# Seven products for four in the y w_in stage, weight scales by block, another order: a single-core chain of linear attention, a gated product and SoLU with layer norm

## The chip, the cores and the metric

The kernel runs on one core of a Trainium2 chip. The core has TensorE (matmuls, from SBUF into the eight banks of PSUM), VectorE, ScalarE, GpSimd and a queue for DMAs on SyncE; they run side by side and wait for each other by semaphores. The profile calls them PE (its weight loads PEld), DVE, ACT, POOL and SP. The metric is the device time of one execution in microseconds (us).

## The reference, cut to what matters

Decaying linear attention over 2 x 8 heads gives x, 1536 tokens by 512; then two dense stages follow:

```python
a = x @ w_a                      # 512 -> 1536
b = x @ w_b
y = (a * b) @ w_out              # 1536 -> 512
h = y @ w_in                     # 512 -> 1024
e = np.exp(h - h.max(-1, keepdims=True))
solu = h * e / (e.sum(-1, keepdims=True) + 1e-9)
ln = (solu - mean) / np.sqrt(var + 1e-6) * g_ln
out = ln @ moe2_w_out            # 1024 -> 512
```

Inputs and output are float32.

## The kernel before, in words

Every dense operand is scaled by a power of two and split in a high and a low half of 16 bits; a product is three matmuls, high by high, high by low and low by high (`mm3`, L139). The tokens are 12 chunks of 128, in three blocks t of 512 (four token blocks j each).

The parts of the work are generators, named by a letter, that issue a few instructions and yield. `ORDER`, a string of 1228 words, resumes them one by one; since all five queues are issued by hand, this string is the order of every engine. The letters: G a load, A scores, K and Q decays, C the products of a chunk, O and T its state, X the scale of a pair of chunks, Y their split; D decodes a block of weights (two ScalarE passes, a VectorE pass `fab`, then its largest magnitudes `st_ab`), P makes a scale out of these, S splits the block (ScalarE the high half, VectorE the low half `wab`). A scale is a spread of the largest values by matmuls (`pm`) and three short VectorE instructions (`pow2`).

The products x w_a and x w_b run for two feature blocks of each pair as plain products (L: banks `pa`, `pb`, 24 groups of 12 matmuls of 512 columns in all; one L is halved to 256 columns), and for the other four pairs by Strassen's scheme with seven products (R: banks `rA`, `rB`, `rC`, on sums of halves of x, `tt` and `xt`, and of the weights, H and E, `ws`). One scale for w_a and one for w_b serve a pair of feature blocks, so a plain block waits until both blocks of its pair are decoded.

M is (a b) w_out (bank `py`, 432 matmuls of 512 columns). U makes the scale of y for a block t, V splits it: `halve` reads the bank on ScalarE and again on VectorE. N (`L3`) makes h for a token block in two banks `ph`, 4 x 3 matmuls each, 288 of 512 columns for the 12 token blocks, and goes on with softmax and norm: VectorE finds the largest value in both banks (L601), ScalarE takes the exponential, VectorE multiplies by h out of the banks (L616), takes moments (L619, L621), GpSimd works out the inverse root (L625 to L630), VectorE applies it (L633). Z splits the result and turns it (by DMA, for the last two blocks by TensorE), W multiplies by the last weights (bank `po`) and stores.

PSUM has eight banks, taken in turn by all of these (`bank`). A tile that is still read keeps its bank, and the matmul that gets the bank next waits for it.

Of the kernel before, what the change touches and what calls it, by code (L numbers as in the profile page):

```python
# [756 lines left out]
```

## Time and profile before

| | us |
|---|---|
| median of 3 runs (least to most) | 462.25 (461.88 to 462.25) |
| the profiled execution | 462.19 |
| its span, first to last instruction | 460.4 |
| TensorE busy | 443.3 |
| VectorE, ScalarE, GpSimd busy | 316.7, 221.5, 179.7 |

The profiled execution agrees with the median to 0.06 us; 1.8 us of it lie outside the span. Engine times in the page are merged busy times; a matmul's duration there is longer than the step to the next one, because matmuls overlap, so the price of a matmul is read from the chain of waits (time of a run of them by their number).

### The profile page before, as it was taken

Reading aid. Unit: us, or ns where it says so; the run is one execution under the profiler, and the core shown is the slowest. Engines: PE = TensorE matmul, PEld = TensorE weight load, DVE = VectorE, ACT = ScalarE, POOL = GpSimd, SP = SyncE. Lnnn points to the kernel's source line nnn. Section 1 sums busy time; section 2 is a strip of 40 time slices with the busy share of each in tenths; the row PEclk is TensorE's granted clock in tenths of the full one; section 3 lists DMA queues with packets and bytes.
Section 4 is the critical chain, followed back from the end, with each engine's and each line's share of the span. In section 5 each row is a group of like instructions: output and inputs, shape, how many; then the busy total and the mean of one; then the engine's idle time right before and its main releaser. Section 6 shows DMA issues by size and latency. Waiting matters only on the chain.

```text
span 460.4 us, 7751 instructions
## 1 busy us (share of the span) xinstructions
PE 443.3 (96%) x3102; PEld 274.5 (60%) x3102; DVE 316.7 (69%) x572; ACT 221.5 (48%) x361; POOL 179.7 (39%) x221
## 2 busy tenths in 40 slices
PE   5777999999999999999999999999999999999996
PEld 5666645568887865888874444444444445544442
DVE  5898898799766337887798668287926799533710
ACT  1546564458536545897796354033503244322421
POOL 5756368547825505337325100003430142803230
PEclk9998999999999999999999999999999999999999
DMA  8974535650000013313606430001320020523051
GB/s 312 374 312 192 230 116 216 219 229 2 0 3 0 1 49 135 113 72 107 244 16 236 167 145 1 0 2 40 43 57 0 24 46 24 151 56 91 1 159 46
DMA packets 30371, 48.73 MB, mean 106 GB/s; under 512 B 22272, under 2 KB 22528, under 8 KB 27008
## 3 DMA queue, kind: packets, MB, share of 16 engines
...
## 4 chain that ended last, share of the span: by engine, by line
PE 90%; DVE 6%; ACT 2%; issue 1%; DMA 1%; POOL 1%; SPq 0%; ACTq 0%; DVEq 0%
PE py L139 20%; PE po L139 14%; PE ph L139 14%; PE rA L139 13%; PE rB L139 7%; PE pa L139 6%; PE pb L139 6%; PE rC L139 3%; PE px L235 2%; PE pss L214 2%; PE px L229 1%; DVE fab L337 1%; DVE sc L219 1%; DMA qk<-in_qk_dram 1%; ACT xh L284 1%
## 5 line engine op out<-in xcount | busy, mean ns | idle before, releaser
L139 PE MATMUL py<-g,wo 128*128 128x512 f16 x432 | 94.3, 379 | 0.0
L139 PEld LDWEIGHTS <-wab 128*128 128x128 f16 x744 | 71.9, 98 | 35.5 <-issue 1.1
L139 PEld LDWEIGHTS <-wo 128*128 128x128 f16 x432 | 42.2, 98 | 50.3
L139 PE MATMUL ph<-wi,yh 128*128 128x512 f16 x288 | 63.9, 379 | 0.0
L139 PE MATMUL po<-wo,zT 128*128 128x512 f16 (+1 forms) x312 | 62.9, 363 | 0.0
L139 PEld LDWEIGHTS <-ws 128*128 128x128 f16 x576 | 55.9, 98 | 7.8 <-DVE ws L437 0.7
L625 POOL TENSOR_SCALAR st<-st 128x1 f32<-128x1 f32 x12 | 3.4, 285 | 125.9 <-DVE st L621 125.8
L139 PEld LDWEIGHTS <-zT 128*128 128x128 f16 x312 | 30.5, 98 | 31.7
L139 PEld LDWEIGHTS <-yh 128*128 128x128 f16 x288 | 28.1, 98 | 33.2
L541 POOL TENSOR_TENSOR g<-c,g 128x512 f16<-128x512 f32 x24 | 31.2, 1314 | 35.2 <-ACT g L539 35.1
L608 ACT ACTIVATE e<-ph,st,ch 128x512 f32<-128x512 f32 x24 | 18.4, 773 | 43.7 <-DVE st L603 31.8
L139 PE MATMUL rA<-xt,ws 128*128 128x256 f16 x288 | 35.4, 273 | 0.0
L139 PE MATMUL pa<-xh,wab 128*128 128x512 f16 (+1 forms) x156 | 33.3, 363 | 0.0
L139 PE MATMUL pb<-xh,wab 128*128 128x512 f16 (+1 forms) x156 | 33.3, 363 | 0.0
L497 ACT ACTIVATE p<-rA 128x512 f32<-128x512 f32 x36 | 21.3, 598 | 19.9 <-PE rA L139 19.7
L335 ACT ACTIVATE raw<-raw 128x1024 f32<-128x1024 f32 x26 | 29.8, 1146 | 0.0
L648 POOL TENSOR_TENSOR zr<-e,zr 128x512 f16<-128x512 f32 x20 | 23.3, 1189 | 14.5 <-ACT zr L644 10.2
L601 DVE TENSOR_REDUCE st<-ph 128x1 f32<-128x512 f32 x24 | 16.0, 682 | 17.5 <-PE ph L139 17.5
L110 DVE TENSOR_REDUCE ym<-py 128x1 f32<-128x512 f32 x12 | 8.3, 689 | 26.1 <-PE py L139 26.1
L689 ACT ACTIVATE ob<-po,glm 128x512 f32<-128x512 f32 (+1 forms) x13 | 8.5, 655 | 30.7 <-PE po L139 23.0
L530 POOL TENSOR_TENSOR c<-p,p 128x512 f32<-128x512 f32 x12 | 16.9, 1409 | 14.4 <-ACT p L497 14.4
L382 ACT ACTIVATE yh<-py,sy 128x512 f16<-128x512 f32 x12 | 7.3, 688 | 31.3 <-DVE sy L130 31.3
(129 smaller groups left out, 765.0 us busy)
## 6 DMA issues: line engine op xcount, KB each, us to landing
...
zT<-zr SPq DMA_TRANSPOSE x20, 2.8
...
```

The source lines that it names most:

```text
L110: nc.vector.tensor_reduce(out=dst, in_=src, axis=AX.X, op=ALU.max, apply_absolute_value=True)
L139: nc.tensor.matmul(o, w[a], x[b], start=start and i == 0, stop=stop and i == 2, skip_group_check=True)
L214: nc.tensor.matmul(pss[e][:, a * P:(a + 1) * P], t[r, 1, a], t[r, 0, a], start=True, stop=True, skip_group_check=True)
L235: nc.tensor.matmul(o[r, a * P:(a + 1) * P], v[:, 2 * a + e], sc[n][e][:, a], start=(c == 0 and a == 0), stop=True, skip_group_check=True)
L335: nc.scalar.activation(hi.bitcast(F32), hi.bitcast(F32), AF.Prelu, scale=2.0 ** -112, alpha=2.0 ** 32)
L497: nc.scalar.activation(r, o, AF.Copy, scale=2.0 ** -28)
L530: nc.gpsimd.tensor_sub(c1[:, 1], p167, p5)
L541: nc.gpsimd.tensor_sub(g[:, 1], c[:, :, 0], g[:, 0])
L601: nc.vector.tensor_reduce(out=st[:, z:z + 1], in_=ph[z], axis=AX.X, op=ALU.max)
L608: nc.scalar.activation(e[z], ph[z], AF.Exp, bias=st[:, 2:3], scale=c, accum_out=st[:, 3 + z:4 + z])
L648: nc.gpsimd.tensor_sub(lo, e[z], hi)
L689: nc.scalar.activation(ob, po, AF.Copy, scale=scl["glm"][:, KB:])
```

## The change

- `L3(t, i)` now makes h for two token blocks, 2i and 2i+1, together: y by halves of its 512 features and pairs of token blocks, w_in by halves, seven products of 6 matmuls in three banks `hA`, `hB`, `hC`, in place of 2 x 24 matmuls. There are 6 of these. Three partial results per pair are copied out by ScalarE (`kept`), two are joined by VectorE (`h`), one by GpSimd (`h22`). The even block's h is then a tile in SBUF; of the odd block's one half is in SBUF, the other stays in the bank `hA`.
- `norm(t, j)` is the rest of the former `L3`. For the even block it works on 1024 columns at once.
- y is written out by ScalarE in float32 (`yf`), split by ScalarE and GpSimd (`yh`), added up by GpSimd (B, `sums_y`) and the sums split by ScalarE and VectorE (F, `yt`). The sums of w_in are made and split once (I and k, `si`, `wsi`).
- The plain pairs 0 and 1 of w_a and w_b get a scale for each feature block (p, `scale_f`), with tables twice as long, and the two blocks of w_out for them are split by halves.
- 22 matmuls on a constant are issued first on TensorE (`warm`).
- Some scales are made with a top of 12 in place of 14. `ORDER` has 1330 words and is another string throughout.

```diff
-ORDER = ("G,qk,1 G,qk,0 G,qk,6 G,kv,1 G,kv,0 G,qk,3 G,kv,3 G,qk,4 G,ab,2 G,ab,1 G,qk,2 G,kv,2 G,qk,5 A,1 A,0 A,1 A,1 Q,6 A,6 A,0 K,1 C,1 A,0 K,1 A,6 C,0 C,1 K,0 "
+ORDER = ("G,qk,0 G,kv,0 G,qk,1 G,ab,0 G,kv,1 G,qk,2 G,kv,2 G,qk,3 G,kv,3 G,ab,1 G,qk,4 G,kv,4 G,qk,5 G,kv,5 A,0 K,0 K,0 A,0 T,0 A,0 C,0 T,0 O,2 A,1 C,0 D,ab,0 "
...
+WARM = 22
...
+    pw = bank("warm")
+    for _ in range(WARM):
+        nc.tensor.matmul(pw[:, :P], identb, identb, start=True, stop=True, skip_group_check=True)
...
-        amax(stab[:, f // 2, :, f % 2] if nm == "ab" else wst[nm][:, f], x)
-        yield
+        amax(stab[:, f // 2, f % 2] if nm == "ab" else wst[nm][:, f], x)
+        yield
+    def scale_f(f):
+        return pow2(stab[:, f // 2, f % 2], 2, sab[:, :, f], TOP)
...
-            amax(r2, stab[:, f])
-            yield
-            yield from pow2(r2, 2, sab[:, :, f], TOP)
+            amax(r2, stab[:, f].rearrange("p e z -> p z e"))
+            yield
+            yield from pow2(r2, 2, sab[:, :, 2 * f], TOP)
...
-        yield from pow2(r, 1, s)
+        yield from pow2(r, 1, s, TOP if nm == "i" else 14)
...
+            k = 2 * len(PLAINW)
+            both = sab[:, 0, k:].rearrange("p (f e) z -> p f e z", e=2)
+            nc.vector.tensor_copy(both[:, :, 1], both[:, :, 0])
...
+        if nm == "i" or nm == "o" and f not in PLAINW:
+            s = scl["ro"][:, 2 * f:2 * f + 1] if nm == "o" else scl[nm][:, 0]
...
-        ss = sab[:, 0, f // 2] if nm == "ab" else scl["glm"][:, 2 * f:2 * f + 2]
+        ss = sab[:, 0, f if f // 2 in PLAINW else f - f % 2] if nm == "ab" else (scl["ro"] if nm == "o" else scl["glm"])[:, 2 * f:2 * f + 2]
...
-        ys[t] = [t_k("yh", (P, 2, 2, W), F16) for _ in range(2)]
-        yield from pow2(r, 1, s)
+        yield from pow2(r, 1, s, TOP)
...
     def split_y(t, d):
-        return halve(pys.pop((t, d)), sy[t][:, 0], ys[t][d // 2][:, d % 2])
+        if t not in yf:
+            yf[t] = [t_k("yf", (P, 2, W)) for _ in range(2)]
+        f = yf[t][d // 2][:, d % 2]
+        nc.scalar.activation(f, pys.pop((t, d)), AF.Copy, scale=sy[t][:, 0])
+        yield
+        if t not in ys:
+            ys[t] = [t_k("yh", (P, 2, 2, W), F16) for _ in range(2)]
+        c = slice(0, W if d // 2 else W // 2)
+        y = ys[t][d // 2][:, d % 2]
+        nc.scalar.copy(y[:, 0, c], f[:, c])
+        yield
+        nc.gpsimd.tensor_sub(y[:, 1, c], f[:, c], y[:, 0, c])
+        yield
+    yfs, yt = {}, {}
+    def halves(x):
+        return [x[..., k * (W // 2):(k + 1) * (W // 2)] for k in range(2)]
+    def sums_y(t):
+        (y11, y21), (y12, y22) = (halves(yf[t][h]) for h in range(2))
+        yfs[t] = [t_k("yu", (P, 2, W))]
+        u = halves(yfs[t][0])
+        nc.gpsimd.tensor_add(u[0], y21, y22)
+        yield
+        nc.gpsimd.tensor_sub(u[1], u[0], y11)
+        yield
+        yfs[t].append(t_k("yv", (P, 2, W)))
+        v = halves(yfs[t][1])
+        nc.gpsimd.tensor_sub(v[0], y11, y21)
+        yield
+        nc.gpsimd.tensor_sub(v[1], u[1], y12)
+        yield
+    def split_ys(t, k):
+        src = yfs[t][k]
+        if t not in yt:
+            yt[t] = {}
+        y = yt[t][k] = t_k("yt", (P, 2, 2, W), F16)
+        nc.scalar.copy(y[:, :, 0], src)
+        yield
+        nc.vector.tensor_sub(y[:, :, 1], src, y[:, :, 0])
+        yield
+    ifs = [None] * 4
+    def sums_i(k):
+        ifs[k] = t_k("si", (P, 2, W))
+        for r in range(2):
+            def w(h, z):
+                return fw["i", 2 * h + r][:, z]
+            if k == 0:
+                nc.gpsimd.tensor_sub(ifs[0][:, r], w(0, 0), w(0, 1))
+            elif k == 1:
+                nc.gpsimd.tensor_add(ifs[1][:, r], w(1, 1), ifs[0][:, r])
+            elif k == 2:
+                nc.gpsimd.tensor_sub(ifs[2][:, r], w(1, 1), w(0, 1))
+            else:
+                nc.gpsimd.tensor_sub(ifs[3][:, r], w(1, 0), ifs[1][:, r])
+            yield
+    def split_si(k):
+        src = ifs[k]
+        w = wt["si", k] = t_k("wsi", (P, 2, 2, W), F16)
+        s = scl["i"][:, 0]
+        nc.scalar.activation(w[:, :, 0], src, AF.Copy, scale=s)
+        yield
+        nc.vector.scalar_tensor_tensor(out=w[:, :, 1], in0=src, scalar=s, in1=w[:, :, 0], op0=ALU.mult, op1=ALU.subtract)
+        yield
...
-    def L3(t, j):
+    hs, sts = {}, {}
+    def L3(t, i):
         y = ys[t]
...
+        def product(o, y, c, w, start, stop):
+            for r in range(2):
+                wh, wl = w(r)
+                mm3(o, (y[:, r, 0, c], y[:, r, 1, c]), (wh, wl), start and r == 0, stop and r == 1)
...
+        A, Bk = bank("hA"), bank("hB")
+        product(A, y[0], at[0], wi(0, 0), True, False)
+        yield
+        product(Bk, yt[t][0], ss[0], si(0), True, False)
+        yield
+        p1 = kept("p1", A)
+        yield
+        product(A, yt[t][0], ss[1], si(1), False, False)
+        yield
+        p5 = kept("p5", Bk)
+        yield
+        product(Bk, yt[t][1], ss[1], wi(1, 1), False, True)
+        yield
+        p16 = kept("p16", A)
+        yield
+        product(A, yt[t][1], ss[0], si(2), False, False)
+        yield
+        h = t_k("h", (P, 2, W))
+        nc.vector.tensor_sub(h[:, 1], p16, Bk)
+        yield
+        C = bank("hC")
+        product(C, y[1], at[0], wi(1, 0), True, True)
+        yield
+        p167 = kept("p167", A)
+        yield
+        product(A, y[1], at[1], si(3), False, True)
+        yield
+        nc.vector.tensor_add(h[:, 0], p1, C)
+        hs[t, 2 * i] = h
+        yield
+        r = t_row("h22", (P, W))
+        nc.gpsimd.tensor_sub(r, p167, p5)
+        hs[t, 2 * i + 1] = (A, r)
+        yield
+    def norm(t, j):
         ch = scl["ch", t, j]
         c, cn = ch[:, 0:1], ch[:, 1:2]
-        js = slice(place(t, j) * P, (place(t, j) + 1) * P)
-        ph = [bank(f"ph{z}") for z in range(2)]
         st = sm.tile([P, 16], F32, name="st")
-        for z in range(2):
-            for kk in range(KD):
-                w = wt["i", kk * 2 + z]
-                mm3(ph[z], (y[kk // 2][:, kk % 2, 0, js], y[kk // 2][:, kk % 2, 1, js]), (w[:, 0], w[:, 1]), kk == 0, kk == KD - 1)
-            yield
-        for z in range(2):
-            nc.vector.tensor_reduce(out=st[:, z:z + 1], in_=ph[z], axis=AX.X, op=ALU.max)
-            if z == 1:
-                nc.vector.tensor_scalar(st[:, 2:3], st[:, 0:1], st[:, 1:2], cn, op0=ALU.max, op1=ALU.mult)
+        h = hs[t, j]
+        whole = j % 2 == 0
+        zs_ = [slice(0, 2)] if whole else [0, 1]
+        src = [h] if whole else h
...
+        for z, x in zip(zs_, src):
+            k = 0 if whole else z
+            nc.scalar.activation(e2[:, z], x, AF.Exp, bias=st[:, 2:3], scale=c, accum_out=st[:, 3 + k:4 + k])
+        yield
+        if whole:
+            nc.vector.tensor_scalar(st[:, 5:6], st[:, 3:4], 1e-9, None, op0=ALU.add)
+        else:
+            nc.vector.scalar_tensor_tensor(out=st[:, 5:6], in0=st[:, 3:4], scalar=1e-9, in1=st[:, 4:5], op0=ALU.add, op1=ALU.add)
...
+        for z, x in zip(zs_, src):
+            nc.vector.scalar_tensor_tensor(out=e2[:, z], in0=e2[:, z], scalar=st[:, 7:8], in1=x, op0=ALU.mult, op1=ALU.mult)
...
+        for z in [slice(0, 2)] if whole else range(2):
+            nc.vector.tensor_scalar(e2[:, z], e2[:, z], st[:, 8:9], r, op0=ALU.subtract, op1=ALU.mult)
+            if whole or z == 1:
...
-             "D": decode, "P": scale_w, "S": split_w, "J": sums_x, "H": sums_w, "E": split_s, "R": R1, "L": L1, "M": L2, "U": scale_y, "V": split_y, "N": L3, "Z": Z, "W": L4}
+             "D": decode, "P": scale_w, "p": scale_f, "S": split_w, "J": sums_x, "H": sums_w, "E": split_s, "R": R1, "L": L1, "M": L2, "U": scale_y, "V": split_y, "B": sums_y, "F": split_ys, "I": sums_i, "k": split_si, "N": L3, "n": norm, "Z": Z, "W": L4}
```

How the change stands on the engines, at three places. VectorE in the head of the kernel, in front of the first low half of a plain weight block, before (`xh` and `tt`: splits and sums of x; `sab`: weight scales):

```order
L337 SCALAR_TENSOR_TENSOR fab<-raw,fab 128x1024
L110 TENSOR_REDUCE st_ab<-fab 128x2
L110 TENSOR_REDUCE r_480<-st_ab 128x2
L288 SCALAR_TENSOR_TENSOR xh<-px,sx_400,xh 128x2x128 x2
L127 TENSOR_REDUCE pm<-pm 128x2
L129 TENSOR_SCALAR pm<-pm 128x2
L130 TENSOR_SCALAR sab<-pm 128x2
L260 TENSOR_TENSOR state<-old,pst 128x256
L110 TENSOR_REDUCE xst<-px 128x1
L406 SCALAR_TENSOR_TENSOR wab<-fab,sab,wab 128x512 x2
```

and with the change:

```order
L313 SCALAR_TENSOR_TENSOR tt<-px,sx_363,tt 128x256
L297 SCALAR_TENSOR_TENSOR xh<-px,sx_271,xh 128x2x128 x2
L297 SCALAR_TENSOR_TENSOR xh<-px,sx_363,xh 128x2x128 x2
L131 TENSOR_REDUCE pm<-pm 128x2
L133 TENSOR_SCALAR pm<-pm 128x2
L134 TENSOR_SCALAR sab<-pm 128x2
L269 TENSOR_TENSOR state<-old,pst 128x256 x2
L228 TENSOR_TENSOR sc<-pss,mask 128x512
L421 SCALAR_TENSOR_TENSOR wab<-fab,sab,wab 128x512 x2
```

Before, three passes `fab` stand in front of the first `wab`; now one does, and the splits of two pairs of chunks stand there in its place.

GpSimd between the last product of the gated stage and the first norm, before:

```order
L541 TENSOR_TENSOR g<-c_2711,g 128x512
L541 TENSOR_TENSOR g<-c_2965,g 128x512
L625 TENSOR_SCALAR st<-st 128x1
L626 TENSOR_TENSOR st<-st,half 128x1
L627 TENSOR_TENSOR st<-st 128x1
```

and with the change (`si` are sums of w_in, `yu` and `yv` sums of y, `yh` its low halves):

```order
L556 TENSOR_TENSOR g<-c_2647,g 128x512
L657 TENSOR_TENSOR si<-fi 128x512 x2
L659 TENSOR_TENSOR si<-fi,si 128x512 x2
L663 TENSOR_TENSOR si<-fi,si 128x512 x2
L661 TENSOR_TENSOR si<-fi 128x512 x2
L626 TENSOR_TENSOR yu<-yf 128x2x256
L628 TENSOR_TENSOR yu<-yu,yf 128x2x256
L612 TENSOR_TENSOR yh<-yf,yh 128x512 x2
L612 TENSOR_TENSOR yh<-yf,yh 128x256 x2
L632 TENSOR_TENSOR yv<-yf 128x2x256
L634 TENSOR_TENSOR yv<-yu,yf 128x2x256
```

GpSimd had nothing there between the two stages; now the sums stand there, ahead of what the first N of a block reads.

VectorE in the last stage, before (`ph`: the two banks of one token block):

```order
L601 TENSOR_REDUCE st<-ph_4251 128x1
L601 TENSOR_REDUCE st<-ph_4252 128x1
L603 TENSOR_SCALAR st<-st,ch_3218 128x1
L610 SCALAR_TENSOR_TENSOR st<-st 128x1
L611 RECIPROCAL st<-st 128x1
L612 TENSOR_TENSOR st<-st,ch_3218 128x1
L616 SCALAR_TENSOR_TENSOR e<-e,st,ph_4251 128x512
L616 SCALAR_TENSOR_TENSOR e<-e,st,ph_4252 128x512
L619 BN_STATS bn<-e 128x6 x2
L621 BN_AGGR st<-bn 128x2
```

and with the change (`h<-p,hC` and `h<-p,hB` join partial results of two different pairs of blocks):

```order
L729 TENSOR_TENSOR h<-p_3838,hC 128x512
L749 TENSOR_REDUCE st<-h 128x1
L751 TENSOR_SCALAR st<-st,ch_3184 128x1
L773 BN_AGGR st<-bn 128x2
L720 TENSOR_TENSOR h<-p_4150,hB 128x512
L749 TENSOR_REDUCE st<-hA 128x1
L760 TENSOR_SCALAR st<-st 128x1
L763 RECIPROCAL st<-st 128x1
L764 TENSOR_TENSOR st<-st,ch_3184 128x1
L768 SCALAR_TENSOR_TENSOR e<-e,st,h 128x1024
```

The joins are new on VectorE, the work of several blocks is mixed, and a bank `hA` is read here long after its last matmul was issued.

## Rows read from the trace of the kernel before

**Rows 1.** The page's first part: busy time, share of the span and instructions of each engine.
```profile
PE 443.3 (96%) x3102; PEld 274.5 (60%) x3102; DVE 316.7 (69%) x572; ACT 221.5 (48%) x361; POOL 179.7 (39%) x221
```

**Rows 2.** The chain that ended last, in order of time: start us, us, what.
```profile
69.86 0.62 PE pst L254 x16
...
73.17 1.09 PE pss L214 x16
...
76.96 1.02 PE px L229 x16
...
99.66 0.61 PE rB L139 x4
...
101.58 1.31 PE rB L139 x12
...
130.74 0.22 PE pm L119 x2
...
239.44 33.67 PE py L139 x156
...
456.58 0.69 ACT ob L689
```

**Rows 3.** Busy by stretch: window; PE, PEld, DVE, ACT, POOL (instructions); TensorE clock, DMA, GB/s.
```profile
0.00:20.00 20.00, 12.57 (x164) 11.38 (x164) 12.83 (x29) 5.27 (x11) 12.99 (x27) 1.00 0.90 359
20.00:40.00 20.00, 14.92 (x210) 12.85 (x210) 19.71 (x36) 13.64 (x20) 14.63 (x17) 0.87 0.81 325
40.00:60.00 20.00, 19.74 (x210) 14.30 (x209) 16.68 (x32) 11.84 (x19) 9.24 (x11) 0.96 0.35 135
60.00:80.00 20.00, 20.00 (x141) 10.24 (x139) 18.21 (x29) 10.20 (x17) 14.17 (x13) 1.00 0.46 178
80.00:100.00 20.00, 19.61 (x126) 10.50 (x124) 16.03 (x19) 11.72 (x17) 13.01 (x10) 1.00 0.62 229
...
280.00:300.00 20.00, 20.00 (x95) 9.04 (x94) 10.18 (x27) 4.26 (x4) 0.00 (x0) 1.00 0.00 0
```

**Rows 4.** VectorE in order of time: start us, us, engine line op out<-in.
```profile
59.55 0.68 DVE L110 TENSOR_REDUCE xst<-px 128x1 f32<-128x512 f32 x1
60.15 0.67 DVE L469 TENSOR_TENSOR asb<-asb,pb 128x512 f32<-128x512 f32 x1
...
62.12 0.43 DVE L127 TENSOR_REDUCE pm<-pm 128x2 f32<-128x256 f32 x1
...
62.90 1.34 DVE L337 SCALAR_TENSOR_TENSOR fab<-raw,fab 128x1024 uint32<-128x1024 uint32 x1
```

**Rows 5.** Groups by form: busy us, mean ns of one, idle before them.
```profile
L337 DVE SCALAR_TENSOR_TENSOR fab<-raw,fab 128x1024 uint32<-128x1024 uint32 x12 | 17.3, 1440 | 5.8 <-ACT raw L335 5.8
...
L219 DVE TENSOR_TENSOR sc<-pss,mask 128x512 f32<-128x512 f32 x24 | 15.8, 682 | 2.6 <-PE pss L214 2.5
...
L110 DVE TENSOR_REDUCE st_ab<-fab 128x2 f32<-128x1024 f32 x12 | 14.6, 1215 | 0.2
...
L406 DVE SCALAR_TENSOR_TENSOR wab<-fab,sab,wab 128x512 f16<-128x512 f32 x16 | 13.7, 886 | 0.1
...
L288 DVE SCALAR_TENSOR_TENSOR xh<-px,sx,xh 128x256 f16<-128x256 f32 x24 | 10.2, 474 | 0.2 <-ACT xh L284 0.2
...
L304 DVE SCALAR_TENSOR_TENSOR tt<-px,sx,tt 128x256 f32<-128x256 f32 x12 | 5.8, 479 | 0.9 <-ACT xh L284 0.7
L424 POOL TENSOR_TENSOR s<-fab 128x512 f32<-128x512 f32 x4 | 5.6, 1390 | 0.0
...
L689 ACT ACTIVATE ob<-po,glm 128x256 f32<-128x256 f32 x2 | 1.0, 476 | 3.1 <-PE po L139 3.1
```

**Rows 6.** The stretch in which VectorE works on one token block's softmax alone; columns as above.
```profile
406.40:418.40 12.00, 12.00 (x58) 5.45 (x56) 5.95 (x13) 2.80 (x6) 1.51 (x6) 1.00 0.06 23
```

**Rows 7.** Line L633, ns least/median/most; then VectorE and GpSimd in one stretch.
```profile
L633 DVE TENSOR_SCALAR e<-e,st x24: 494/542/1381, 313.8 to 441.2; 128x512 f32<-128x512 f32 x24
...
370.11 2.65 DVE L633 TENSOR_SCALAR e<-e,st 128x512 f32<-128x512 f32 x2
...
370.02 2.45 POOL L648 TENSOR_TENSOR zr<-e,zr 128x512 f16<-128x512 f32 x2
```

More of the change, by code (lines that the diff above doesn't have):

```diff
@@ L321, in body @@
     fw, wt, scl = {}, {}, {}
-    sab = const.tile([P, 2, KA // 2, 2], F32, name="sab")
+    sab = const.tile([P, 2, KA, 2], F32, name="sab")
     def decode(nm, f):
@@ L364, in scale_w @@
             oi = scl["oi"] = const.tile([P, 1], F32, name="oi")
-            nc.vector.tensor_scalar(oi, scl["ro"][:, KA + 1:], scl["o"][:, 1], 2.0 ** (55 - 7), op0=ALU.mult, op1=ALU.mult)
+            nc.vector.tensor_scalar(oi, scl["ro"][:, 2 * KA + 1:], scl["o"][:, 1], 2.0 ** (55 - 7), op0=ALU.mult, op1=ALU.mult)
             nc.vector.tensor_scalar(oi, oi, s[:, 1], None, op0=ALU.mult)
         if nm == "o":
+            k = 2 * len(PLAINW)
+            both = sab[:, 0, k:].rearrange("p (f e) z -> p f e z", e=2)
+            nc.vector.tensor_copy(both[:, :, 1], both[:, :, 0])
             turn(sab)
-            n = KA // 2
+            n = KA
             s4 = scl["ro"] = const.tile([P, 2 * n + 2], F32, name="s4")
@@ L431, in split_s @@
         w = wt["s", p, k] = t_k("ws", (P, 2, 2, W), F16)
-        ss = sab[:, 0, p]
+        ss = sab[:, 0, 2 * p]
         for z in range(2):
@@ L580, in scale_y @@
         yield
+    yf = {}
     def split_y(t, d):
-        return halve(pys.pop((t, d)), sy[t][:, 0], ys[t][d // 2][:, d % 2])
+        if t not in yf:
[11 more added lines that the diff above has]
+        yield
@@ L586, in body, with wi, si, kept @@
+    def split_si(k):
[6 more added lines that the diff above has]
+        yield
     es, zs = {}, {}
-    def L3(t, j):
+    hs, sts = {}, {}
+    def L3(t, i):
         y = ys[t]
+        at = [slice(place(t, 2 * i + e) * P, (place(t, 2 * i + e) + 1) * P) for e in range(2)]
+        ss = [slice(k * W // 2 + i * P, k * W // 2 + (i + 1) * P) for k in range(2)]
+        def product(o, y, c, w, start, stop):
+            for r in range(2):
+                wh, wl = w(r)
+                mm3(o, (y[:, r, 0, c], y[:, r, 1, c]), (wh, wl), start and r == 0, stop and r == 1)
+        def wi(h, z):
+            return lambda r: (wt["i", 2 * (2 * h + r) + z][:, 0], wt["i", 2 * (2 * h + r) + z][:, 1])
+        def si(k):
+            return lambda r: (wt["si", k][:, r, 0], wt["si", k][:, r, 1])
+        def kept(nm, o):
+            r = t_row(nm, (P, W))
+            nc.scalar.copy(r, o)
+            return r
+        A, Bk = bank("hA"), bank("hB")
[32 more added lines that the diff above has]
+        yield
@@ L600, in L3 @@
-        for z in range(2):
-            nc.vector.tensor_reduce(out=st[:, z:z + 1], in_=ph[z], axis=AX.X, op=ALU.max)
-            if z == 1:
-                nc.vector.tensor_scalar(st[:, 2:3], st[:, 0:1], st[:, 1:2], cn, op0=ALU.max, op1=ALU.mult)
+        h = hs[t, j]
+        whole = j % 2 == 0
+        zs_ = [slice(0, 2)] if whole else [0, 1]
+        src = [h] if whole else h
+        for z, x in enumerate(src):
+            if whole:
+                x = x.rearrange("p z n -> p (z n)")
+            nc.vector.tensor_reduce(out=st[:, z:z + 1], in_=x, axis=AX.X, op=ALU.max)
+            if z == len(src) - 1:
+                nc.vector.tensor_scalar(st[:, 2:3], st[:, 0:1], st[:, z:z + 1], cn, op0=ALU.max, op1=ALU.mult)
@@ L606, in L3 @@
         e = [e2[:, z] for z in range(2)]
-        for z in range(2):
-            nc.scalar.activation(e[z], ph[z], AF.Exp, bias=st[:, 2:3], scale=c, accum_out=st[:, 3 + z:4 + z])
+        for z, x in zip(zs_, src):
+            k = 0 if whole else z
+            nc.scalar.activation(e2[:, z], x, AF.Exp, bias=st[:, 2:3], scale=c, accum_out=st[:, 3 + k:4 + k])
         yield
-        nc.vector.scalar_tensor_tensor(out=st[:, 5:6], in0=st[:, 3:4], scalar=1e-9, in1=st[:, 4:5], op0=ALU.add, op1=ALU.add)
+        if whole:
+            nc.vector.tensor_scalar(st[:, 5:6], st[:, 3:4], 1e-9, None, op0=ALU.add)
+        else:
+            nc.vector.scalar_tensor_tensor(out=st[:, 5:6], in0=st[:, 3:4], scalar=1e-9, in1=st[:, 4:5], op0=ALU.add, op1=ALU.add)
         nc.vector.reciprocal(st[:, 6:7], st[:, 5:6])
@@ L614, in L3 @@
         bn = sm.tile([P, 2, 6], F32, name="bn")
-        for z in range(2):
-            nc.vector.scalar_tensor_tensor(out=e[z], in0=e[z], scalar=st[:, 7:8], in1=ph[z], op0=ALU.mult, op1=ALU.mult)
+        for z, x in zip(zs_, src):
+            nc.vector.scalar_tensor_tensor(out=e2[:, z], in0=e2[:, z], scalar=st[:, 7:8], in1=x, op0=ALU.mult, op1=ALU.mult)
             yield
@@ L631, in L3 @@
         yield
-        for z in range(2):
-            nc.vector.tensor_scalar(e[z], e[z], st[:, 8:9], r, op0=ALU.subtract, op1=ALU.mult)
-            if z == 1:
+        for z in [slice(0, 2)] if whole else range(2):
+            nc.vector.tensor_scalar(e2[:, z], e2[:, z], st[:, 8:9], r, op0=ALU.subtract, op1=ALU.mult)
+            if whole or z == 1:
                 es[t, j] = e
```

2 lines of the change are left out of this document (removed), and 97 rows, old and new, of the table ORDER.

## The prediction

> **What bounds the kernel now.** I read the busy line of the page first: TensorE is busy for 443.3 us, 96% of the span, VectorE for 69%, GpSimd for 39% [rows 1]. Then the chain of waits in order of time [rows 2]: its rows are TensorE's nearly throughout, so the end is set by the sum of the matmuls plus what TensorE loses at both ends. It gives the price of a matmul, since one row is a back-to-back run: 33.67 us for 156 matmuls of 512 columns is 0.2158 us each, a group of 12 costs 2.59; 12 of 256 columns cost 1.31, a group of scores (`pss`) 1.09, of values or state reads (`px`) 1.02, a state update (`pst`) 0.62, one spread of a scale (`pm`) 0.11 [rows 2]. Third, the windows of 20 us show who is late: in the head VectorE is busy for 19.71 of 20 us from 20 to 40 and 18.21 from 60 to 80, while TensorE there issues short groups, at a mean granted clock of 0.87 from 20 to 40; at 280 TensorE is full at clock 1.00, GpSimd idle, ScalarE at 4.26 and VectorE at 10.18 of 20 [rows 3]. So the head is set by VectorE and loads, the rest by TensorE.
>
> How much the head loses: counted from the program, TensorE has 10 `pss`, 17 `px`, 10 `pst`, 14 spreads, 5 groups of 256 columns and 14 of 512 ahead of the first `rB`: 10.9 + 17.3 + 6.2 + 1.5 + 6.6 + 36.3 = 78.8 us. That `rB` starts at 99.66 [rows 2]. 20.9 us are lost there.
>
> **The change part by part.** The sum is made against the profiled execution, 462.19, which stands 0.06 under the median of 462.25.
>
> *Seven products for h.* 12 x 24 = 288 matmuls of 512 columns become 6 x 7 x 6 = 252. 36 x 0.2158 = **-7.8**. They lie in the stage where TensorE never waits, so this comes through whole if the new operands are in time.
>
> By the Trainium skill ("TensorE: Matmul & The Clock Gate", section "Back-to-back issue gap") a stream of 512-column matmuls keeps about 131 ns each, which would make this estimate -4.7 and the time 457.3. The trace has 215.8 ns over 156 of them in a row at a granted clock of 1.00, so the measurement decides and -7.8 stands.
>
> *Scales for each feature block of the plain pairs.* Four more spreads, 4 x 0.11 = **+0.4** on TensorE. Their VectorE work (a set of three takes 0.78, from 62.12 to 62.90 [rows 4]) is counted in the head.
>
> *The head in its new order.* I compare what stands on VectorE. First milestone: the first plain product of full width. Before, VectorE has done `xst`, from where such work can go on, by 60.2 [rows 4]. Now, counted from the order, what that product needs differs from this by one `sc` more (0.66), four `xh` (0.43 each) and four `tt` (0.48) more, and one `fab` (1.44), two `st_ab` (1.22) and four `wab` (0.86) fewer [rows 5]: +0.66 + 1.7 + 1.9 - 1.44 - 2.4 - 3.4 = -3.0. So it starts at about 57.2, or at 53.6 if the 3.6 us that VectorE idles from 20 to 60 [rows 3] go too. Second milestone: the first product on `ws`. On from the first one VectorE did 39.4 us before (99.66 - 60.2, idle included) and now has one `sc`, one `xst`, three sets of scales, two `st_ab` and four `wab` more and one `asb` (0.6) fewer: 0.7 + 0.6 + 2.3 + 2.4 + 3.4 - 0.6 = 8.8, so 48.2: 105.4. If the 5.8 us that it idled from 60 to 100 (40 - 34.24 [rows 3]) get filled, 99.6; and 96.0 if the first milestone is at 53.6. TensorE's own work between the two is 41.0 us (80.4 in all up to there, 39.4 up to the first), so it could be there at 57.2 + 41.0 = 98.2. The order has more plain work ready at this place, which is how such idle time is filled; I take 100.0. Lost: 100.0 - 80.4 = 19.6 in place of 20.9, **-1.3**. Bounds: 96.0 gives -5.3, 105.4 gives +4.1. What the first scores wait for is a load, in front of which the 22 constant matmuls stand; hidden by it they cost nothing, and without that cover at most 22 x 0.11 = 2.4.
>
> *The new sums and copies.* GpSimd gets 20 sums of 512 columns, like line L424's at 1.39 [rows 5], 28 us in all, and low halves; ScalarE copies three banks a pair. These stand where GpSimd does nothing and ScalarE has 15.7 of 20 us free [rows 3]: 0 beside TensorE. What may not be hidden is the last mile of each block: between the last scale of y and the first N of that block stand a set of scales (0.8), four copies (about 0.69 each, as `ob` [rows 2], 2.8), four sums (5.6) and a low half (1.4), 10.6 us; TensorE's cover there, counted from the order for block 1, is three groups of 512 and three of 256 columns, 11.7. So it is hidden, by 1.1. Also a bank `hA` is held until the odd block's norm has multiplied out of it. Bounds of all late waits: 0, and 18 if each of the six pairs waits for 3 us (half the 5.95 that a norm takes on VectorE [rows 6]). I take **+0.8**, near the lower end, since before no wait of this kind appears in the stage.
>
> *The tail.* The last copy is half as wide: 0.69 [rows 2] becomes 0.48 [rows 5]: **-0.2**.
>
> Sum: 462.2 - 7.8 + 0.4 - 1.3 + 0.8 - 0.2 = **454.1** us.
>
> **The rivals.** *The head opens altogether.* VectorE loses its idle time in both stretches, the first product on `ws` starts at 96.0, and nothing waits later: 454.1 - 4.0 - 0.8 = 449.3. For it: VectorE idles 7.2 us in the first 20 us too, behind loads [rows 3], and the loads are in another order now. Against it: VectorE was already at 19.71 of 20.
>
> *The late waits take half the gain.* Hand-overs of y miss by 1 to 2 us for each block and banks by some more, 4 to 7 us in all: 458 to 461. For it: the 1.1 us of slack above is worked out with GpSimd alone on its port. Against: it is one place in each of three blocks.
>
> *Slower: VectorE's backlog at the end holds the banks.* By the order TensorE has 25 products of 6 matmuls nearly in a row near the end, with two output groups: 25 x 1.295 + 2 x 5.18 = 42.7 us, 3.57 pairs. VectorE needs for a pair two norms at 5.95 [rows 6] and two joins at 0.67 (as `asb` [rows 4]), 13.2: 47.3, and for the last y two splits of 1024 columns (1.34 each, as `fab`) and four maxima (0.68) [rows 4], 5.4 more. It falls 10.0 us behind, and `hA` of each odd block stays taken for so long. If the remaining banks can't carry that, TensorE waits 10.0, and a last norm beside GpSimd costs 1.6 more (two of L633 in 2.65 while GpSimd worked 2.45 [rows 7], in place of 2 x 0.54): 453.3 + 11.6 = 464.9. It comes out slower from 9.8 us of waits on. For it: GpSimd now works in the very stage where it was mostly idle, and L633 ran from 494 to 1381 ns [rows 7]. Against it: two further `h` tiles are SBUF copies, so that the even block holds no bank. The Trainium skill ("GPSIMD Engine Reference", section "1. Specifications") says that GpSimd shares its SBUF interfaces with VectorE and contends with VectorE's two-port modes and two-input instructions; the spread of L633 agrees with it.
>
> *The change doesn't do what it says*, and TensorE's time stays: the counts exclude it, and only waits that eat the gain exactly would end within 0.2%.
>
> **How the numbers follow.** Something like 0.2% (0.9 us) is about what a measurement of this kernel can tell from no change. The forecast (450.5 to 457.5): 0.50. The head opens altogether (447 to 450.5, or somewhat under): 0.17. Late waits (457.5 to 461.3): 0.18. Within 0.2%: 0.04. The backlog, slower: 0.11. Faster is 0.50 + 0.17 + 0.18 = 0.85. The time is the likeliest case's, 454.1. The range from 447 to 462 leaves out the slower case, and a few hundredths of each neighbour.
>
> **What would show it.** The seven products: 252 matmuls in `hA`, `hB`, `hC` and 36 fewer of 512 columns in all, TensorE's busy time some 7 us less. The head: the first full-width `pa` near 57, the first product on `ws` near 100, VectorE's idle time from 60 to 100 under 2 us. The late waits: in windows from 300 on TensorE is at 20.00 of 20 but for about 1 us; a hand-over that misses shows as a wait of a `hA` or `hB` matmul for GpSimd's low half of y or ScalarE's `yt`, the backlog as a wait of TensorE for VectorE's multiplication out of `hA`. The tail: a last `ob` of 0.48. The prediction is wrong if TensorE's idle time after 100 us exceeds 4 us, or if the first `ws` product starts outside 96 to 105.

## The result, and the profile after

| us | before | changed |
|---|---|---|
| median of 4 runs (least to most) | 462.25 (461.88 to 463.37) | 458.2 (457.71 to 459.15) |
| ratio to before, 95% interval | | 0.9915 (0.9901 to 0.9928) |
| profiled execution, its span | 462.19, 460.4 | 457.83, 456.1 |
| first product on `ws` starts | 98.23 | 102.08 |
| from there to the last copy `ob` | 358.35 | 350.69 |
| from there to the end of the span | 3.82 | 3.33 |

The change made the kernel faster by 4.05 us, half of the 8.1 forecast. The last three lines split the span of the profiled executions: the head became 3.85 us longer, the rest 7.66 shorter, the tail 0.49 shorter: 4.30 in all, as the spans say.

The engines' busy line of the page after, which answers to [rows 1], and the groups of the new products by form (busy us, mean ns | idle before them):

```profile
PE 438.5 (96%) x3092; PEld 273.9 (60%) x3092; DVE 337.7 (74%) x571; ACT 248.5 (54%) x397; POOL 232.2 (51%) x259
```
```profile
L143 PE MATMUL hA<-wsi,yt 128*128 128x512 f16 x72 | 17.3, 379 | 0.0
...
L143 PE MATMUL hA<-wi,yh 128*128 128x512 f16 x36 | 8.8, 379 | 0.0
L143 PE MATMUL hB<-wi,yt 128*128 128x512 f16 x36 | 8.8, 379 | 0.0
L143 PE MATMUL hB<-wsi,yt 128*128 128x512 f16 x36 | 8.8, 379 | 0.0
L143 PE MATMUL hC<-wi,yh 128*128 128x512 f16 x36 | 8.7, 380 | 0.0
L143 PE MATMUL hA<-wsi,yh 128*128 128x512 f16 x36 | 8.7, 379 | 1.4 <-ACT p L699 1.4
```

72 and five times 36 are the 252 matmuls, and only one of these groups ever waits, for 1.4 us. Windows of 20 us, columns as in [rows 3]:

```profile
0.00:20.00 20.00, 14.57 (x186) 12.55 (x186) 12.39 (x23) 4.19 (x6) 12.09 (x26) 0.91 0.91 355
20.00:40.00 20.00, 16.89 (x210) 14.96 (x210) 18.12 (x37) 12.31 (x23) 16.10 (x17) 0.83 0.55 213
40.00:60.00 20.00, 15.77 (x230) 13.73 (x228) 16.61 (x37) 11.03 (x19) 13.79 (x16) 0.83 0.55 223
60.00:80.00 20.00, 20.00 (x164) 11.21 (x161) 17.33 (x34) 10.00 (x16) 6.10 (x6) 1.00 0.55 211
80.00:100.00 20.00, 20.00 (x107) 9.38 (x105) 18.71 (x24) 14.01 (x21) 14.43 (x10) 1.00 0.60 211
280.00:300.00 20.00, 20.00 (x94) 9.04 (x93) 18.47 (x21) 11.38 (x11) 6.36 (x5) 1.00 0.00 0
360.00:380.00 20.00, 18.55 (x87) 8.31 (x86) 15.56 (x23) 11.44 (x20) 16.67 (x21) 1.00 0.30 64
```

From 60 us on TensorE is full but for 1.45 us near 373. Below 60 it is neither full nor at full clock: 0.83 from 20 to 60, where before had 0.87 and 0.96. TensorE's waits between 5 and 60 us (total, times, longest), first of the changed kernel, then of before:

```profile
PE pst L263 <- POOL kd L208: 3.6, 3, 2.7
PE pm L123 <- DVE xst L114: 2.7, 1, 2.7
PE px L244 <- DMA kv<-in_kv_dram: 2.5, 1, 2.5
PE px L238 <- DVE state L269: 1.6, 1, 1.6
```
```profile
PE pm L119 <- DVE r L110: 3.1, 1, 3.1
PE px L235 <- DVE sc L219: 2.5, 2, 2.3
PE px L229 <- DVE state L260: 1.0, 1, 1.0
PE pst L254 <- POOL kd L199: 0.7, 1, 0.7
```

The first one now is for GpSimd's `kd`, the other large ones for VectorE's maxima and state and for a load. Behind them the clock is low. The third column from the end is the granted clock; first two stretches of the changed kernel, then two of before:

```profile
26.00:32.00 6.00, 5.63 (x56) 5.10 (x58) 5.83 (x17) 5.64 (x10) 5.84 (x7) 0.50 0.39 156
53.00:59.00 6.00, 4.43 (x40) 3.67 (x40) 5.79 (x16) 3.17 (x7) 5.84 (x8) 0.50 0.02 4
```
```profile
22.00:24.00 2.00, 2.00 (x19) 1.78 (x18) 2.00 (x4) 2.00 (x3) 2.00 (x3) 0.50 0.04 14
39.00:41.00 2.00, 2.00 (x22) 1.67 (x20) 1.81 (x2) 1.34 (x3) 2.00 (x3) 0.50 0.40 164
```

0.50 is 1.2 of 2.4 GHz. By windows of 1 us the low clock lasted about 17 us in the changed kernel (it also had one at 12 to 15) and 7 in before.

The one wait behind the head, on four engines in order of time (start us, us, engine line op):

```profile
371.48 3.84 POOL L800 TENSOR_TENSOR zr<-e,zr 128x512 f16<-128x512 f32 x3
371.56 1.62 DVE L785 TENSOR_SCALAR e<-e,st 128x1024 f32<-128x1024 f32 x1 [1.17 <-POOL st L782]
373.21 0.62 ACT L796 CAST zr<-e 128x512 f16<-128x512 f32 x1 [2.10 <-DVE e L785]
...
373.74 0.58 ACT L699 COPY p<-hA 128x512 f32<-128x512 f32 x1
...
374.37 0.81 PE L143 MATMUL hA<-wsi,yh 128*128 128x512 f16 x3 [1.45 <-ACT p L699]
```

TensorE waits for a copy of `hA`, which stands on ScalarE behind a cast that waits for VectorE's norm, which waited for GpSimd's `st`. GpSimd had worked on sums and low halves of y until 366.4. The moments (L773) that it needs had been ready earlier, for another norm since 358.75 and for this one since 366.14; it began on the two (L777) at 366.50 and 369.44:

```profile
358.54 0.21 DVE L773 BATCH_NORM_AGGREGATE st<-bn 128x2 f32<-128x12 f32 x1
...
365.93 0.21 DVE L773 BATCH_NORM_AGGREGATE st<-bn 128x2 f32<-128x12 f32 x1
...
366.50 0.19 POOL L777 TENSOR_SCALAR st<-st 128x1 f32<-128x1 f32 x1
...
369.44 0.19 POOL L777 TENSOR_SCALAR st<-st 128x1 f32<-128x1 f32 x1
```

### The profile page after: what moved, and what is told of

It reads as the page before. It is cut to its first block, busy times and chain, and to the rows that moved or that the text cites. A ratio compares the mean times of both kernels' runs of the same rounds, so it can differ in the third digit from the quotient of the medians.

```text
span 456.1 us, 7817 instructions
## 1 busy us (share of the span) xinstructions
PE 438.5 (96%) x3092; PEld 273.9 (60%) x3092; DVE 337.7 (74%) x571; ACT 248.5 (54%) x397; POOL 232.2 (51%) x259
## 4 chain that ended last, share of the span: by engine, by line
PE 86%; DMA 4%; POOL 4%; DVE 2%; ACT 1%; issue 1%; SPq 0%; ACTq 0%; POOLq 0%
PE py L143 20%; PE rA L143 14%; PE po L143 13%; PE pa L143 7%; PE rB L143 7%; PE pb L143 7%; PE hA L143 5%; DMA qk<-in_qk_dram 4%; PE rC L143 3%; PE hB L143 2%; PE pss L223 2%; PE px L238 2%; PE px L244 1%; PE hC L143 1%; PE pst L263 1%
## 5 line engine op out<-in xcount | busy, mean ns | idle before, releaser
L489 POOL TENSOR_TENSOR g<-asb,g 128x512 f16<-128x512 f32 x12 | 16.0, 1334 | 34.2 <-ACT g L487 34.2
L800 POOL TENSOR_TENSOR zr<-e,zr 128x512 f16<-128x512 f32 x20 | 24.7, 1255 | 12.0 <-ACT zr L796 12.0
L545 POOL TENSOR_TENSOR c<-p,p 128x512 f32<-128x512 f32 x12 | 15.7, 1306 | 20.6 <-ACT p L512 19.5
L143 PEld LDWEIGHTS <-yt 128*128 128x128 f16 x144 | 14.0, 98 | 16.9 <-DVE yt L644 0.3
L550 DVE SCALAR_TENSOR_TENSOR c<-c 128x512 f32<-128x512 f32 x24 | 20.1, 847 | 4.9 <-ACT c L547 4.6
L346 DVE SCALAR_TENSOR_TENSOR fab<-raw,fab 128x1024 uint32<-128x1024 uint32 x12 | 15.5, 1294 | 7.4 <-ACT raw L344 7.4
L418 ACT ACTIVATE wab<-fab,sab 128x512 f16<-128x512 f32 (+1 forms) x24 | 14.4, 640 | 11.0 <-DVE sab L134 11.0
L421 DVE SCALAR_TENSOR_TENSOR wab<-fab,sab,wab 128x512 f16<-128x512 f32 (+1 forms) x24 | 18.9, 822 | 1.1 <-ACT wab L418 1.1
L796 ACT CAST zr<-e 128x512 f16<-128x512 f32 x20 | 11.4, 616 | 14.2 <-DVE e L785 14.2
```

Of the source, the lines that this page charges most:

```text
L143: nc.tensor.matmul(o, w[a], x[b], start=start and i == 0, stop=stop and i == 2, skip_group_check=True)
L346: nc.vector.scalar_tensor_tensor(out=flat, in0=hi, scalar=3, in1=flat, op0=ALU.logical_shift_left, op1=ALU.bitwise_or)
L418: nc.scalar.activation(w[:, z, 0, c], src[:, z, c], AF.Copy, scale=ss[:, z:z + 1])
L421: nc.vector.scalar_tensor_tensor(out=w[:, z, 1, c], in0=src[:, z, c], scalar=ss[:, z:z + 1], in1=w[:, z, 0, c], op0=ALU.mult, op1=ALU.subt ...
L489: nc.gpsimd.tensor_sub(g[:, 1], a, g[:, 0])
L545: nc.gpsimd.tensor_sub(c1[:, 1], p167, p5)
```

## The experiments

All start from the changed kernel but e14; an edit of `ORDER` is shown by the piece of the string that it changes. In each profiled execution I took the start of the first product on `ws` and the time from there to the last `ob`, called the rest: 350.69 in the changed kernel.

**a0_after**, no edit.

> The changed kernel unchanged, as the measure for the three beside it on one chip: 457.5 to 459, and again 353.5 to 354 us from the first product on ws to the end of the span, since that stretch was 353.9, 353.6 and 353.8 in the profiles of the changed kernel, of the one without constant matmuls and of the one with the other order in the head, while the start of that product moved between 100.4 and 102.2.

457.93 (456.04 to 459.94), 0.9911 (0.9879 to 0.9943). First `ws` product at 100.33, rest 350.84. e2 and e4 below have the same head too, and in their profiles that product starts at 103.23 and 103.02. So what varies from run to run of one program lies in the head, and it is up to 2.9 us between single profiles; a difference of 1 or 2 us between two profiled heads tells little.

```profile
100.33 1.76 PE L143 MATMUL rB<-xt,ws 128*128 128x256 f16 x12
```
```profile
103.23 1.47 PE L143 MATMUL rB<-xt,ws 128*128 128x256 f16 x12
```

**e1_no_warm**

```diff
-WARM = 22
+WARM = 0
```

> The changed kernel without its 22 constant matmuls at the start. Theory 1 (the head waits for loads): the first scores start at 4.5 to 4.9 us either way, and TensorE waits 2.5 us for the first kv load at 9.8 us and later again, so a lower clock in the first scores (16 of them took 1.44 us with the constant matmuls; 48 took 5.50 in the kernel before, against 3.27 at full clock) is hidden by these waits: 458.2, within 0.5. Rival (the clock of the first scores counts): up to 2 us slower, 459 to 460.

457.66 (455.68 to 458.4); the first scores start at 4.56 where they started at 4.55. No difference that these runs can tell: the 22 matmuls are hidden, and no use of them shows. Nor do they fix the pace of what follows: the first 16 scores took 1.44 us in the profile of the changed kernel but 2.08 in a0's, the same program, and 2.08 here.

```profile
4.55 1.44 PE L223 MATMUL pss<-qk 64*128 64x128 f32 x16 [0.39 <-DMA qk<-in_qk_dram]
```
```profile
4.66 2.08 PE L223 MATMUL pss<-qk 64*128 64x128 f32 x16 [0.49 <-DMA qk<-in_qk_dram]
```

The granted clock of these windows is 1.00 in all three profiles, so it doesn't tell them apart; the reason stays open.

**e2_c_twice**

```diff
         product(C, y[1], at[0], wi(1, 0), True, True)
+        product(C, y[1], at[0], wi(1, 0), True, True)
```

> The changed kernel with the product in hC issued twice for each of the six pairs: 36 matmuls of 512 columns more, exactly the number that the change took away, in the same stage. Theory 1 (TensorE sets the time of that stage, the seven products gave their whole gain, and the head lost the rest): 36 x 0.216 = 7.8 us more, less the 1.4 us wait that they may cover: 464.6 to 466.0. Rival (the stage is now bound by VectorE, ScalarE or GpSimd for part of its length, so part of the gain never arrived): the added matmuls fill waits and cost clearly less, 460 to 463.

465.29 (463.76 to 467.02), 7.1 over the changed kernel. The rest is 356.65, 5.96 more: the 7.8 less the 1.45 wait, which is gone there (TensorE waits for nothing after 100 us), to 0.4. 36 matmuls of that stage are worth their price.

**e4_copy_first**: `N,2,0` (the copy) ahead of `Z,0,0` (the cast).

```diff
-Z,0,1 N,2,0 Z,0,0 N,2,0 Z,0,1 N,2,0 Z,0,0 N,2,0
+Z,0,1 N,2,0 N,2,0 Z,0,1 N,2,0 Z,0,0 Z,0,0 N,2,0
```

> The changed kernel with one ScalarE copy (p167 of a pair of the last block, near 372 us) ahead of a ScalarE cast that waits for VectorE and GpSimd. Theory 1: the only wait of TensorE after 100 us, 1.45 us, goes, and nothing behind it waits: 456.7 to 457.2. Rival (VectorE and GpSimd are behind there, the wait comes back at the next pair): 458.0 to 458.4.

456.2 (454.59 to 457.36); rest 349.28, 1.4 less, and TensorE's only wait after 100 us is now this one:

```profile
PE po L143 <- DMA zT<-zr: 0.3, 1, 0.3
```

**e3_state_first**: on VectorE, both `xst` and the state addition ahead of two `tt` and the `xh`, the next scale behind them.

```diff
-T,6 J,2 D,ab,4 J,2 A,8 Q,8 Y,4 J,2 p,2 C,7 J,2 J,2 C,6 D,ab,4 Y,5 J,2 X,3 X,3 X,3 Q,9 T,6 Y,6
+T,6 C,7 C,6 T,6 J,2 D,ab,4 J,2 A,8 Q,8 X,3 Y,4 J,2 p,2 X,3 X,3 J,2 J,2 D,ab,4 Y,5 J,2 Q,9 Y,6
```

> The changed kernel with, in the head near 50 us, the two maxima of x (xst), the state addition and the spread of the next x scale ahead of the third and fourth sum tt and of the splits xh on VectorE; the same instructions. Theory 1 (TensorE's waits of 2.7 and 1.6 us at 50 to 55 come from VectorE's order, since VectorE idles beside them, and not from the amount of its work): the state read starts about 3 us earlier and as much shows in the time, 455 to 456.5. Rival (VectorE's amount of work sets the head, as in the forecast): the wait only moves to the next product, 457.7 to 458.7.

456.72 (455.42 to 458.32). The 2.7 us wait for `xst` is 0.3, but the state read now waits 1.4 for `xh`, which still reads its bank. First `ws` product at 101.05. The median is 1.2 us under a0's, of 3 expected, and the intervals of the two overlap (0.9875, 0.9857 to 0.9893, and 0.9911, 0.9879 to 0.9943): half right at most.

**e7_loads**

```diff
-G,qk,1 G,ab,0 G,kv,1 G,qk,2 G,kv,2 G,qk,3 G,kv,3 G,ab,1 G,qk,4 G,kv,4 G,qk,5 G,kv,5
+G,qk,1 G,kv,1 G,ab,0 G,qk,2 G,kv,2 G,qk,3 G,kv,3 G,qk,4 G,kv,4 G,qk,5 G,kv,5 G,ab,1
```

> The changed kernel with another order of loads: the first weight block behind kv,1 and the second one behind kv,5, with its decoding on ScalarE moved behind the first split of weights. Theory 1 (the waits of 2.5 us for kv at 9.8 and of 2.7 for GpSimd behind qk at 23.5 come from 1 MB weight loads standing ahead of 0.5 MB loads that are wanted earlier): these two waits fall by 3 to 5 us together, the time to 454 to 456. Rival (GpSimd's chain of old, qd and kd is as late by itself, it waited only 0.8 us for that qk): at most 1 us, 457 to 458.

Two further pieces of the string move the decoding of the second weight block (`D,ab,1`). 458.23 (457.61 to 458.99): nothing gained. TensorE's wait for GpSimd's `kd` fell from 3.6 to 1.6 and the one for the load is gone, yet the first `ws` product is at 102.40: the stretches at clock 0.50 are still there (26 to 33 and 53 to 60), and waits of 0.5 to 1.1 for other things came up.

**e8_three**: the edits of e7, e3 and e4 together.

> The three edits of order together: loads, state and maxima first on VectorE near 50 us, and the one copy ahead near 372 us. Theory 1 (TensorE's waits add up one to one in the time): the sum of the three single gains, 451 to 454. Rival (VectorE's amount of work in the head comes next and takes back what the loads give): 455 to 456.5.

455.82 (454.02 to 456.45), within the rival's range; its reason isn't shown. Between the first scores and the first `ws` product TensorE waits 5.85 us, 4.79 less than in the changed kernel, but that product starts only 1.0 earlier. The low clock at 26 to 33 and 53 to 61 is still there, but by windows of 1 us it lasted 13.7 us in all, less than the 17, so it doesn't explain what is missing. Part of that lies ahead of 10 us, where the first 16 scores took 2.08 us here as in a0; the rest stays open.

**e9_fill**: constant matmuls in TensorE's queue where it waits, in columns that are overwritten or not read (T: state update, P: spread of a weight scale, C: state read).

```diff
+FILL = {"T5": 22, "P2": 22, "C8": 12}
...
+    def busy(o, n):
+        for _ in range(n):
+            nc.tensor.matmul(o, identb, identb, start=True, stop=True, skip_group_check=True)
...
+        busy(pstb[:, 3 * P:], FILL.get(f"T{n}", 0))
...
+        busy(pm[:, 3 * P:], fill)
...
+        busy(o[:, :P], FILL.get(f"C{n}", 0))
...
+        return pow2(stab[:, f // 2, f % 2], 2, sab[:, :, f], TOP, FILL.get(f"P{f}", 0))
```

> The changed kernel with 22 constant matmuls more ahead of the state update that waited 2.73 us for GpSimd at 23.5 us, 22 ahead of the two spreads before the 2.66 us wait for the maxima at 50.2, and 12 ahead of the state read that waited 1.57 us at 53.2. They are put into columns that are overwritten or not read; no order is changed. Theory 1 (what the head loses beyond its waits is TensorE's clock: the granted clock was 0.50 from 26 to 32 and from 53 to 59 us, each time behind such a wait, 2 stretches of 3.4 us in the kernel before): with TensorE busy in the waits the clock stays at 1.00 there, about 6.5 us of work at the half clock in the first stretch and 4.8 in the second take half the time: up to 5.6 us less, 452.5 to 455. Rival (the low clock comes whatever TensorE does in the waits, or what follows is held by other engines anyway): 457.5 to 459 and the same two stretches at 0.50.

455.84 (455.28 to 455.9), 0.9851 (0.9832 to 0.9871). The granted clock is 1.00 throughout the profile, and the four runs lie within 0.6 us of each other:

```profile
26.00:32.00 6.00, 4.35 (x70) 3.69 (x72) 5.83 (x16) 5.64 (x9) 6.00 (x8) 1.00 0.42 168
53.00:59.00 6.00, 4.78 (x87) 3.99 (x85) 5.83 (x15) 3.17 (x7) 5.86 (x8) 1.00 0.01 1
```
```profile
59.38 2.76 PE L149 MATMUL pa<-xh,wab 128*128 128x512 f16 x12
...
100.31 1.47 PE L149 MATMUL rB<-xt,ws 128*128 128x256 f16 x12
```

2.1 to 2.4 us came back in the median, against a0 and against the first measurement, and not 5.6. The first `ws` product stands 1.77 earlier than in the profile of the changed kernel, but no earlier than in a0's. At full clock TensorE is ready sooner and waits in more places (0.3 to 1.2 us each, for a `qk` load, `sc`, `state`, `kd`).

**e10_three_fill**: e8 with two such fillings.

```diff
+FILL = {"T5": 14, "P2": 12, "C8": 0}
```

> The kernel with the three edits of order, with 14 constant matmuls ahead of the state update that waits for GpSimd near 24 us and 12 ahead of a spread at 50 us. Theory 1 (the three edits took 4.8 us of waits out of the head, and only 1 us came through to the first full-width product, since two stretches of 6.7 us at clock 0.50 stayed): without them 3 to 6 us less, 450 to 453. Rival: 455 to 456.5 with both stretches as they were.

455.15 (453.61 to 457.17). A stretch at 0.50 from 31 to 33 stayed, behind a wait of 1.1 for VectorE. Less than expected, and these runs can't tell it from e8 or e9.

**e11_fill_copy**: e9 with e4's edit.

> The kernel with constant matmuls in TensorE's waits (455.84, clock 1.00 throughout the head) and the one ScalarE copy ahead near 372 us, which alone gave 456.2 against 457.93. Theory 1 (the two losses lie in different stretches and add up): 455.8 less the 1.45 us wait, 454.2 to 454.8. Rival (one covers the other): 455.5 to 456.

454.81 (453.77 to 455.14), 0.9823 (0.9804 to 0.9843): first `ws` product at 99.29, rest 349.42. 1.4 under e4 and 1.0 under e9: the two gains add up in the main, and this is the lowest median here. The filling doesn't hold the runs together every time: these four span 1.4 us, and the six of e12, with the same filling, 4.8, the slowest at a granted clock of 0.985.

**e12_more_vector**: e11 with more work on VectorE.

```diff
+        if nm == "ab" and f in (0, 2):
+            amax(stab[:, f // 2, f % 2], x)
```

> The same kernel with two maxima st_ab of 1.21 us issued twice on VectorE, at 17 and at 36 us: 2.4 us more work on VectorE in front of the first full-width product. The forecast counted the head as VectorE's work, row by row: then 2.4 us more than the kernel beside it, 456.6 to 457.2. Theory 1 (VectorE waits for other engines for 11.8 of the first 60 us; the head is a chain through loads, GpSimd, TensorE and VectorE's order): less than half of it, 454.4 to 455.4.

456.1 (454.79 to 459.61): 1.3 over e11, and 0.84 at the first full-width product (59.20 and 58.36), for 2.4 added. The median lies between both expectations: some of VectorE's added work shows in the time, but its runs (454.79 to 459.61) don't settle how much.

**e6_old_head**: the old order's first 250 words, then what they leave of the new one.

```diff
-    for word in ORDER.split():
+    for word in OLD_HEAD + REST_OF_NEW:
```

> The changed kernel with the order of its head undone: the first 250 words of the order string of before (a spread for each of two feature blocks where one stood for the pair), and then what is left of the new string in its order. Theory 1 (the new order of the head is what loses 2 to 3 us on TensorE; the rest is sound): the wait of TensorE in the first 60 us falls from 15 to about 13 us and the time to 455 to 457, if the seam adds no wait. Rival (the new order of the head is not worse, the 3.5 us that the forecast missed are lost elsewhere): 458 or more with TensorE's waits in the head as they were.

473.16. The seam decides: a spread beyond it waits 9.7 us for VectorE, so the time says nothing. Up to 60 us the old order gives the old head: groups of 512 columns start at 48.92 and 59.47, and at 48.66 and 59.21 in the kernel before.

**e13_fill_late** (e9 without the filling at 24 us) and **e14_before_fill** (the kernel before with 26 constant matmuls ahead of its spread at 33 us).

```diff
-FILL = {"T5": 22, "P2": 22, "C8": 12}
+FILL = {"T5": 0, "P2": 22, "C8": 12}
```

```diff
-            yield from pow2(r2, 2, sab[:, :, f], TOP)
+            yield from pow2(r2, 2, sab[:, :, f], TOP, 26 if f == 0 else 0)
```

> The changed kernel with constant matmuls only in the waits at 50 to 55 us (22 ahead of the two spreads, 12 ahead of the state read), none at 24 us. Theory 1 (each stretch at clock 0.50 comes from the waits just before it): the stretch near 26 to 32 us stays, the one at 53 to 59 us is gone, and about half of e9_fill's gain of 2.1 us: 456.5 to 457.3. Rival (the added matmuls work in another way): both stretches go or both stay.

> The kernel before with 26 constant matmuls ahead of the spread that waited 3.12 us for VectorE at 33 us, behind which the granted clock was 0.50 from 39 to 41 us. Theory 1 (every kernel pays for its waits with the clock): that stretch goes and the one at 22 to 24 us stays; of the 3.4 us at half clock up to 1.7 come back, 460.5 to 461.8, and the changed kernel's loss in the head is one of more and longer such stretches. Rival (VectorE sets what follows at 40 us in the kernel before): the clock is 1.00 there and the time stays at 462 to 462.7.

e13: 456.43 (455.24 to 460.16). In its profile, that of its slowest run, the early stretch is there as expected, the late one is shorter (55 to 58) but not gone; 1.4 us of the wait for `xst` and 1.0 of another for VectorE stayed open. e14: 462.38 (460.37 to 463.36), 0.9982 (0.9966 to 0.9999). The 26 matmuls took 1.63 us, 63 ns each and not the 110 that I had counted, so half of the wait stayed, and so did the low clock behind it:

```profile
33.04 1.63 PE L115 MATMUL pm<-identb 128*128 128x128 bf16 x26
36.24 0.29 PE L124 MATMUL pm<-identb,r 128*128 128x128 bf16 x2 [1.57 <-DVE r L110]
```

So e14 doesn't answer its question, and what the kernel before would gain at full clock stays open.

## Why the prediction was wrong

**Seven products (-7.8) and the scales (+0.4): right.** The counts are those forecast, and e2 shows the price of 36 matmuls to 0.4 us. The rest agrees. By the forecast's own counts 80.4 us of TensorE's work stand ahead of the first `ws` product where 78.8 did; 0.4 of that are the new spreads, so 1.2 moved out of the rest. With the 7.8, and 0.39 for a wait of before that is gone, less the new wait of 1.45, that makes 7.9, and the rest became 7.66 shorter. (TensorE's busy time fell by 4.8 and not by 7: the 22 constant matmuls alone add 2.5. The prediction's other sum, with -4.7 for the products, comes to 457.2 and not 457.3.)

**The head (-1.3): wrong, and with it the size.** The first `ws` product came 3.85 later by the profiles. Less the 1.6 of work that moved there or is new, the time lost in the head rose from 19.4 to 21.7, +2.3 in place of -1.3. Two steps of the forecast failed.

The first is a row misread: "That `rB` starts at 99.66 [rows 2]". That row holds 4 of 12 matmuls; the first 8 stood before it:

```profile
98.23 1.04 PE L139 MATMUL rB<-xt,ws 128*128 128x256 f16 x8
...
99.66 0.61 PE L139 MATMUL rB<-xt,ws 128*128 128x256 f16 x4 [0.39 <-DVE ws L437]
```

So the kernel before lost 19.4 and not 20.9 there, which made the term 1.4 too good.

The second is "So it starts at about 57.2", for the first full-width product, from VectorE's rows added up. It started at 61.14; at 59.4 in a0:

```profile
61.14 2.77 PE L143 MATMUL pa<-xh,wab 128*128 128x512 f16 x12
...
102.08 1.63 PE L143 MATMUL rB<-xt,ws 128*128 128x256 f16 x12
```

From it to `ws` it is 40.94, and 40.93 in a0 and e12: the 41.0 of TensorE's own work, with TensorE full from 60 to 100. The forecast had this path, 57.2 + 41.0 = 98.2, as a bound and took 100.0 by VectorE's rows, 42.8 after the first product. These 1.9 too many hid half of the 3.9 by which the first product was missed; that 100.0 was only 2.1 off (0.3 in a0) is luck.

The first product's start is no sum over one engine. Nor did the sum begin at its like: before, the first product of 512 columns stands at 48.66, and 60.2 is a place in VectorE's queue.

```profile
48.66 2.76 PE L139 MATMUL pa<-xh,wab 128*128 128x512 f16 x12
```

In the changed kernel VectorE is idle for 12.9 of the first 60 us (60 less 12.39, 18.12 and 16.61), TensorE waits in turn for loads, GpSimd and VectorE's order (e3), and each of its longer waits is followed by work at half the clock. e9 takes the low clock away and changes no order, and its median is 2.1 under a0's: the low clock costs time. But its first full-width product still starts at 59.38, 2.2 after the forecast, and the profiled run of a0, at 456.24 one of its two fastest, starts it at 59.40 with 10 us at low clock in place of 17. So 2.2 of the 3.9 stay at a granted clock of 1.00, where TensorE waits for one engine after the other, and what part of the other 1.8 is the clock isn't shown. The forecast had no term for the low clock, though 0.87 stood in [rows 3]. The Trainium skill ("TensorE: Matmul & The Clock Gate", section "Why this matters for your kernels") asks to leave no long idle gaps between bursts of matmuls, lest throughput drop in mid-kernel. The trace agrees in kind: the low clock comes behind waits of 2.73 us, and of 2.66 and 1.57 close together.

**Late waits (+0.8): right in kind, 1.45 in size** (e4 takes 1.4 out of the rest). The place was another one: not the hand-over of y to its own products but ScalarE's order behind a norm that GpSimd's queue, with the sums in it, delayed. VectorE's pass took 1.62 there beside GpSimd; the same form took 0.81 at 348 us, with GpSimd idle:

```profile
348.08 0.81 DVE L785 TENSOR_SCALAR e<-e,st 128x1024 f32<-128x1024 f32 x1
```

That is the contention of [rows 7], and 0.8 of the 1.45 at most.

**The tail (-0.2): 0.5.** The copy went from 0.69 to 0.47; the end behind it took 0.27 less as well, which I had not counted.

**The rivals.** "The late waits take half the gain" gave 458 to 461, and 458.2 lies in it, but by another mechanism: 1.45 us late and the rest in the head. VectorE's backlog at the end did not show: no wait of TensorE for a multiplication out of `hA`. Of the signs that the prediction named, VectorE's idle time from 60 to 100 was 4.0 and not under 2 (40 less 17.33 and 18.71); neither sign of being wrong appeared (1.45 us idle after 100, `ws` at 102.08), since both left more room than the forecast was wrong by.

Against the forecast of -8.1: misread start 1.4, `ws` product later than 100.0 by 2.1 (0.3 in a0's profile), late waits 0.6, tail -0.3: 3.8 together, where the profiled execution lies 3.7 over the forecast (457.83 less 454.1). What remains open is which single wait of the head would have to go (e3 and e7 each took one away and others came up), and how the loss divides between waits and clock.
